# The last two tiles' output product in seven half-size products, and the four narrow tiles' in plain blocks

## The chip, the cores and the metric
The kernel runs on one core of one Trainium2 chip. The metric is the device time of one execution in microseconds (us). Before the change it is 1196.68 us, the median of three runs (1196.1, 1196.68, 1197.64).

## The reference, cut to what matters
```python
# u, v: (8, 3008, 256)   z: (8, 3008, 64)   w_in: (256, 2048)   w_out: (2048, 256)
scores = (1 / 3008) * z @ z.T            # per batch, symmetric
attn = maximum(scores, 0) ** 2
x = u * (attn @ v)                       # 24064 tokens of 256
h = x @ w_in
g = h * cos(h)
out = g @ w_out
```

## The kernel before, in words
The 24064 tokens are cut into 48 tiles, six to a batch, numbered m = 0 to 47. A batch has 3008 = 5 x 512 + 448 tokens, so its sixth tile is short. The 64 tokens left over in an even batch are laid into the last tile of the odd batch after it: tiles 11, 23, 35 and 47 have 512 tokens and tiles 5, 17, 29 and 41 have 384 (`mwidth`, line 393). These four are called narrow here. The inputs of the matmuls are 16-bit floats, the sums 32-bit.

The work goes in slots, s = 3 to 48 (the first three have a form of their own). Slot s has two stages:

- **`phase_a(s)`** (line 305): the scores and the product attn @ v of tile s, as two passes of 47 pairs of matmuls (line 258). The first adds up in the two banks M[0] and M[1] of the accumulator memory, the second in one of the three double banks E[0..2]. ScalarE and VectorE then bring the sums out (`gate_sum`, lines 269 and 270) and VectorE or GpSimd multiplies them by u, which gives x(s) (`gate_mul`, lines 286 and 294). In the last slots no scores are left to do. There is no phase_a(48).
- **`phase_b(s)`** (line 582): eight units of h for tile s-1, with the output product y of tile s-2 between them.

A **unit** of h (`emit_h`, line 396) is four matmuls of 512 columns into the next double bank E, taken in turn (line 403), a sine on ScalarE that gives the cosine c (line 411), and one multiplication h * c on VectorE that writes g and frees the double bank (line 414, here "the g operation"). A unit is two of the 16 blocks of g's depth of 2048. The units go in the order 0, 4, 1, 5, 2, 6, 3, 7, which pairs the upper half of the depth (blocks 0 to 7) with the lower (8 to 15). There are two buffers of g, so g(m) takes the place of g(m-2).

The **output product** has two forms.

- Plain (`emit_y`, line 532; `y_block`, line 522): 16 steps of depth times four blocks of 128 tokens, each one matmul with 256 columns, added up in M[0] and M[1]; `store_y` (line 550) then has ScalarE copy both banks out.
- Mixed (`product`, line 464): the 512 tokens by 2048 of g and the 2048 by 256 of w_out are each cut into 2 x 2 parts, and the result's four quarters are made of seven products of parts or of sums of parts, in place of eight. The sums of w_out's parts are made once (w_mix). Those of g's parts are made per tile: `mix_early` (lines 432 and 433, on GpSimd, one call of two operations for each pair of units) writes s1 and overwrites a quarter of g, and `mix_late` (lines 439 and 441, on VectorE during the next phase_a) writes s2 and s4 in two pieces each. s1, s2 and s4 have one buffer. A product is 16 matmuls of 128 columns (line 482); product n goes to M[0] and M[1] in turn, in the order 5, 1, 6, 7, 2, 3, 4 (`order_y`). Products 5 and 1 are copied out by ScalarE (line 501), each of the others is brought out by one VectorE operation that scales and adds (line 495), and two more sums are made on GpSimd (lines 504 and 507). `store_half` starts the output's DMAs on SyncE's queue: one for a half, or three for the second half of a batch's last tile (lines 542 to 544).

A tile is mixed if 1 <= m < 46. A narrow tile is done with halves of 128 tokens, so its seven products are 8 matmuls each, and its middle 128 tokens go through a plain product of their own (`middle`, line 456, matmuls in line 459). Tiles 0, 46 and 47 are plain. The y of tile 47 is `last_y` (line 561): 64 plain matmuls behind the last unit, two blocks of tokens together and then two one after the other, each with a ScalarE copy (line 571) and a DMA (lines 577 to 580).

Nothing plans the order: the schedule is manual, and each engine runs its instructions as the program emits them. In phase_b a list `after` says behind which unit each product or plain step is emitted. Where y is mixed, a unit's g operation is emitted behind the products that stand with that unit, and so behind their line 495 operations on VectorE; where y is plain, ahead of them. Behind a unit 4 to 7, `mix_early` is emitted.

Of the kernel before, what the change touches and what calls it, by code (L numbers as in the profile page):

```python
# [10 lines left out]
FP32 = mybir.dt.float32  # L11
# [3 lines left out]
def kernel(  # L15
# [9 lines left out]
    nc = tc.nc  # L25
    AF = mybir.ActivationFunctionType
    ALU = mybir.AluOpType

    B, S, D = u.shape
    dqk = z.shape[2]  # L30
    Dff = moe_w_in.shape[1]
    P = 128
    H = P // 2
    CW = 512
# [3 lines left out]
    NFT = Dff // P  # L38
    NSLOT = B * NC
# [4 lines left out]
    inv_s2 = (1.0 / float(S)) * (1.0 / float(S))  # L44
# [16 lines left out]
    opool = pool("o", 2)  # L61
    ypool = pool("ysum", 1)
# [40 lines left out]
    def take_e():  # L103
        i = e_order.pop(0)
        e_order.append(i)
        return i
# [286 lines left out]
    def mwidth(m):  # L393
        return 3 * P if m % (2 * NC) == NC - 1 else CW

    def emit_h(m, i):
        W = mwidth(m)
        x = xs[m]
        e = E[take_e()]
        for f in range(2):  # L400
            ft = 2 * i + f
            for k in range(2):
                nc.tensor.matmul(  # L403
                    e[:, f, 0:W],
                    w_in16[:, k, ft * P:(ft + 1) * P],
                    x[:, k, 0:W],
                    start=(k == 0),
                    stop=(k == 1),
                )
        c = cpool.tile([P, 2, CW], FP16, name="c")  # L410
        nc.scalar.activation(c[:, :, 0:W], e[:, :, 0:W], AF.Sin, bias=half_pi, scale=inv_s2)  # L411
        if m not in gs:
            gs[m] = gpool.tile([P, NFT, CW], FP16, name="g")
        return lambda: nc.vector.scalar_tensor_tensor(  # L414
            gs[m][:, 2 * i:2 * i + 2, 0:W], e[:, :, 0:W], 1.0, c[:, :, 0:W], ALU.mult, ALU.mult
        )

    def mixed(m):
        return 1 <= m < NSLOT - 2

    F = NFT // 2
    T = 2 * P

    def halves_of(m):
        n = T if mwidth(m) == CW else P
        return n, slice(0, n), slice(T, T + n)

    def mix_early(m, j):
        g, f = gs[m], slice(2 * j, 2 * j + 2)
        n, up, low = halves_of(m)  # L430
        lower = slice(F + 2 * j, F + 2 * j + 2)
        nc.gpsimd.tensor_tensor(s1[:, f, 0:n], g[:, f, low], g[:, lower, low], ALU.add)  # L432
        nc.gpsimd.tensor_tensor(g[:, f, low], g[:, f, up], g[:, f, low], ALU.subtract)  # L433

    def mix_late(m, which, c):
        g, f = gs[m], slice(4 * c, 4 * c + 4)
        n, up, low = halves_of(m)
        if which == "s2":
            nc.vector.tensor_tensor(s2[:, f, 0:n], s1[:, f, 0:n], g[:, f, up], ALU.subtract)  # L439
        else:  # L440
            nc.vector.tensor_tensor(  # L441
                s4[:, f, 0:n], g[:, F + 4 * c:F + 4 * c + 4, up], s2[:, f, 0:n], ALU.subtract
            )

    def mix_weights():
# [7 lines left out]

    order_y = (5, 1, 6, 7, 2, 3, 4)

    def middle(m):
        acc = M[0][:, 0:D]
        for ft in range(NFT):
            nc.tensor.matmul(  # L459
                acc, gs[m][:, ft, P:T], w_out16[:, ft, :], start=(ft == 0), stop=(ft == NFT - 1)  # L460
            )
        nc.scalar.activation(y_outs[m][0][:, 1, :], acc, AF.Copy, bias=0.0, scale=inv_s2)

    def product(m, n):
        g = gs[m]
        nk, up, low = halves_of(m)
        nk = nk // P
        t = lambda i: w_mix[:, i, :, :]
        left, right = {
            1: (g[:, 0:F, up], w_out16[:, 0:F, 0:P]),  # L470
            2: (g[:, F:, up], w_out16[:, F:, 0:P]),
            3: (s4, w_out16[:, F:, P:D]),
            4: (g[:, F:, low], t(3)),
            5: (s1, t(0)),
            6: (s2, t(1)),
            7: (g[:, 0:F, low], t(2)),
        }[n]
        at = order_y.index(n) + (nk == 1 and n in order_y[4:])
        acc = M[at % 2][:, 0:nk * P]
        for ft in range(F):  # L480
            for k in range(nk):
                nc.tensor.matmul(  # L482
                    acc[:, k * P:(k + 1) * P],
                    left[:, ft, k * P:(k + 1) * P],
                    right[:, ft, :],
                    start=(ft == 0 and k == 0),
                    stop=(ft == F - 1 and k == nk - 1),
                )
        acc = acc.rearrange("p (k d) -> p k d", d=P)
        if n == 5:  # L490
            y_outs[m] = [opool.tile([P, 2, D], FP32, name="o") for i in range(2)]
            y_parts[m] = {}
        c11, c12, c21, c22 = (y_outs[m][i][:, 0:nk, d * P:(d + 1) * P] for i in range(2) for d in range(2))
        parts = y_parts[m]
        add = lambda dst, other: nc.vector.scalar_tensor_tensor(
            dst, acc, inv_s2, other, ALU.mult, ALU.add
        )
        if n in (1, 5, 6):
            parts[n] = ypool.tile([P, 2, P], FP32, name=f"p{n}")[:, 0:nk, :]
        if n in (1, 5):  # L500
            nc.scalar.activation(parts[n], acc, AF.Copy, bias=0.0, scale=inv_s2)
        elif n == 6:
            add(parts[6], parts[1])
            nc.gpsimd.tensor_tensor(c12, parts[6], parts[5], ALU.add)
        elif n == 7:
            add(c21, parts[6])
            nc.gpsimd.tensor_tensor(c22, c21, parts[5], ALU.add)
        elif n == 2:
            add(c11, parts[1])
        elif n == 3:  # L510
            add(c12, c12)
            store_half(m, 0, y_outs[m][0])
        else:
            add(c21, c21)
            store_half(m, 1, y_outs[m][1])

    def y_bank(m, k):
        if m == NSLOT - 1 and k == 3:
            return E[0][:, 0, 0:D]
        return M[k // 2][:, (k % 2) * D:(k % 2 + 1) * D]  # L520

    def y_block(m, ft, k):
        final = m == NSLOT - 1
        nc.tensor.matmul(  # L524
            y_bank(m, k),
            gs[m][:, ft, k * P:(k + 1) * P],
            w_out16[:, ft, :],
            start=(ft == 0 and (k % 2 == 0 or (final and k == 3))),
            stop=(ft == NFT - 1 and (k % 2 == 1 or k == mwidth(m) // P - 1 or (final and k == 2))),
        )  # L530

    def emit_y(m, i):
# [27 lines left out]

    def last_y(m):
        b, J = m // NC, m % NC
        for ft in range(NFT):
            y_block(m, ft, 0)
            y_block(m, ft, 1)
        for k in range(4):
            if k >= 2:
                for ft in range(NFT):
                    y_block(m, ft, k)
            o = opool.tile([P, 2, D], FP32, name="o")  # L570
            nc.scalar.activation(
                o[:, 0, :], y_bank(m, k),
                AF.Copy, bias=0.0, scale=inv_s2,
            )
            t0 = b * S + J * CW + k * P
            if k < 3:
                nc.sync.dma_start(out[t0:t0 + P, :], o[:, 0, :])
            else:
                nc.sync.dma_start(out[t0:t0 + H, :], o[0:H, 0, :])
                nc.scalar.dma_start(out[b * S - H:b * S, :], o[H:P, 0, :])  # L580

    def phase_b(s):
        y, hs = s - 2, [(s - 1, i) for i in (0, 4, 1, 5, 2, 6, 3, 7)]
        if s == 2:
            hs = [(0, i) for i in range(8)] + hs
        for dh in range(len(late_sums)):
            gate_mul(s, 2 - len(late_sums), late_sums.pop(0), nc.gpsimd)
        if mixed(y):
            ys = [lambda n=n: product(y, n) for n in order_y]
            if mwidth(y) < CW:  # L590
                ys.insert(4, lambda: middle(y))
        else:
            ys = [lambda i=i: emit_y(y, i) for i in range(8)]
            ys[7] = lambda f=ys[7]: (f(), store_y(y))
        n = len(hs)
        if n > 8:
            after = (1, 3, 5, 7, 9, 11, 13, 14)
        elif mixed(y):
            after = (0, 1, 2, 3, 4, 5, 6, 6)
        else:  # L600
            after = (0, 1, 2, 3, 4, 5, 6, 6)
        for i, (m, unit) in enumerate(hs):
            times_c = emit_h(m, unit)
            if not mixed(y):
                times_c()
            for f, place in zip(ys, after):
                if place == i:
                    f()
            if mixed(y):
                times_c()  # L610
            if mixed(m) and unit >= 4:
                mix_early(m, unit - 4)
            if i in (1, 3, 5):
                emit_turns((0, 0), 1)

# [153 lines left out]
```

## Time and profile before

| what | before |
|---|---|
| median of the three runs | 1196.68 us |
| the profiled execution | 1196.1 us |
| its span, first to last instruction | 1194.3 us |
| TensorE matmul busy | 1184.6 us |
| VectorE busy | 1008.6 us |
| ScalarE busy | 795.1 us |
| GpSimd busy | 678.4 us |
| granted TensorE clock | 1.000 |

The span is that of the profiled execution, and 1.8 us lie around it. Busy times of different engines run side by side. PE is TensorE's matmuls, PEld its weight loads, DVE VectorE, ACT ScalarE, POOL GpSimd and SP SyncE, whose queue (SPq) starts most DMAs. In the timelines the columns are start, duration (both us from the span's start), engine, line, operation, output<-inputs with shapes, and a count of instructions merged; the bracket holds the idle time before and what ended it. The stages at the end, from the same execution:

| stage | from to (us) | length |
|---|---|---|
| phase_b(46): h of tile 45, y of 44 | 1133.49 to 1146.76 | 13.27 |
| phase_a(47) | 1146.76 to 1155.76 | 9.00 |
| phase_b(47): h of 46, y of 45 | 1155.76 to 1168.92 | 13.16 |
| phase_b(48): h of 47, y of 46 (plain) | 1168.92 to 1182.98 | 14.06 |
| last_y and the last DMAs | 1182.98 to 1194.30 | 11.32 |

### The profile page before, as it was taken

The numbers are of one execution on the slowest core, as the hardware profiler recorded it, in microseconds if no ns is written. First come the engines' busy times: TensorE is split into PE (matmuls) and PEld (weight loads), VectorE is DVE, ScalarE is ACT, GpSimd is POOL, SyncE is SP. The second block draws the span as 40 slices with busy tenths as digits, with TensorE's granted clock in tenths as the row PEclk, the third lists the DMA queues.
The fourth block names the chain that finished last, engine by engine and source line by source line (L and its number), as shares of the span: only waits on it lengthen the run. The fifth ranks groups of instructions, "written<-read, shape, count | busy, mean of one in ns | idle before, by whom it ended". The sixth has DMA issues, their size and how long they took to land.

```text
span 1194.3 us, 28924 instructions
## 1 busy us (share of the span) xinstructions
PE 1184.6 (99%) x11839; PEld 727.2 (61%) x11839; DVE 1008.6 (84%) x1293; ACT 795.1 (67%) x927; POOL 678.4 (57%) x707
## 2 busy tenths in 40 slices
PE   9899999999999999999999999999999999999998
PEld 4556655665566656566556665666656666665566
DVE  6798988888988898888988889888888888888775
ACT  7866666666766676666766676766766666666454
POOL 3186745557565573665647556476565765545450
PEclk9999999999999999999999999999999999999999
DMA  9999898769995699956999459974798838954301
GB/s 159 172 165 163 121 153 127 118 107 137 139 139 104 114 140 157 128 92 113 150 147 132 91 107 156 169 117 77 121 160 154 122 70 122 183 105 89 65 19 54
DMA packets 479861, 147.98 MB, mean 124 GB/s; under 512 B 404208, under 2 KB 479472, under 8 KB 479728
## 3 DMA queue, kind: packets, MB, share of 16 engines
q1 hardware_dynamic: 380752, 112.93, 54.5%
q0 software_dynamic: 97440, 32.78, 28.1%
q8 instruction: 92, 1.51, 0.5%
q10 hardware_dynamic: 1536, 0.43, 0.2%
q14 instruction: 41, 0.34, 0.1%
HBM read 66.32 MB, written 24.64 MB: 76 GB/s over the span
## 4 chain that ended last, share of the span: by engine, by line
PE 97%; ACT 1%; DVE 1%; issue 1%; ACTq 0%; DVEq 0%
PE E L403 27%; PE M L482 23%; PE M L258 20%; PE E L258 19%; PE E L194 5%; PE M L524 2%; ACT r L204 1%; PE M L459 1%; PE E L654 0%; DVE sm L270 0%; PE E L524 0%; DVE A L209 0%; DVE x L286 0%; DVE g L414 0%; PE M L677 0%
## 5 line engine op out<-in xcount | busy, mean ns | idle before, releaser
L411 ACT ACTIVATE c<-E 128x1024 f16<-128x1024 f32 (+1 forms) x384 | 385.6, 1006 | 218.0 <-PE E L403 214.8
L414 DVE SCALAR_TENSOR_TENSOR g<-E,c 128x1024 f16<-128x1024 f32 (+1 forms) x384 | 458.9, 1197 | 66.7 <-ACT c L411 65.7
L204 ACT ACTIVATE r<-E 128x512 f16<-128x512 f32 (+1 forms) x342 | 327.8, 967 | 114.1 <-PE E L194 108.4
L258 PEld LDWEIGHTS <-v 64*128 64x128 f16 x4512 | 246.8, 94 | 232.4 <-issue 20.6
L403 PE MATMUL E<-x,w_in 128*128 128x512 f16 (+1 forms) x1408 | 353.8, 375 | 0.0
L432 POOL TENSOR_TENSOR s<-g 128x512 f16<-128x512 f16 (+1 forms) x180 | 202.9, 1127 | 185.4 <-DVE g L414 138.9
L258 PE MATMUL M<-A,v 64*128 64x512 f16 (+1 forms) x2256 | 284.9, 372 | 2.1 <-ACT sm L269 1.2
L258 PE MATMUL E<-A,v 64*128 64x512 f16 (+1 forms) x2256 | 279.4, 372 | 0.0
L433 POOL TENSOR_TENSOR g<-g 128x512 f16<-128x512 f16 (+1 forms) x180 | 214.2, 1190 | 14.1
L403 PEld LDWEIGHTS <-w_in 128*128 128x128 f16 x1536 | 133.4, 98 | 108.6 <-issue 19.1
L482 PEld LDWEIGHTS <-g 128*128 128x128 f16 x2752 | 168.6, 98 | 39.8
L209 DVE TENSOR_TENSOR A<-r 128x1024 f16<-128x1024 f16 x240 | 173.3, 734 | 15.1 <-ACT r L204 14.3
L286 POOL TENSOR_TENSOR x<-sm,uT 128x512 f16<-128x512 f32 (+1 forms) x43 | 48.5, 1130 | 214.1 <-DVE sm L270 213.9
L482 PEld LDWEIGHTS <-s 128*128 128x128 f16 x2064 | 126.6, 98 | 30.6
L194 PE MATMUL E<-zT 64*128 64x512 f16 (+4 forms) x684 | 130.0, 356 | 0.5 <-ACT zT L647 0.3
L439 DVE TENSOR_TENSOR s<-s,g 128x1024 f16<-128x1024 f16 (+1 forms) x90 | 98.5, 1094 | 2.1 <-POOL s L432 2.1
L482 PE MATMUL M<-w_out,g 128*128 128x128 f16 x1376 | 91.5, 219 | 0.0
L482 PE MATMUL M<-w_mix,g 128*128 128x128 f16 x1376 | 91.5, 219 | 0.0
L482 PE MATMUL M<-w_mix,s 128*128 128x128 f16 x1376 | 91.5, 219 | 0.0
L212 DVE TENSOR_TENSOR A<-r 128x512 f16<-128x512 f16 (+1 forms) x102 | 80.7, 792 | 10.2 <-ACT r L204 9.4
L194 PEld LDWEIGHTS <-zT 64*128 64x128 f16 x684 | 39.3, 94 | 36.7 <-issue 2.2
L441 DVE TENSOR_TENSOR s<-g,s 128x1024 f16<-128x1024 f16 (+1 forms) x90 | 59.4, 662 | 0.0
(58 smaller groups left out, 657.6 us busy)
## 6 DMA issues: line engine op xcount, KB each, us to landing
out_dram<-o SPq DMA_DIRECT2D x87, 256.0 KB, 2.2
v<-in_v_dram POOLq DMA_DIRECT2D x40, 256.0 KB, 9.2
u<-in_u_dram POOLq DMA_DIRECT2D x40, 256.0 KB, 4.8
A<-A SPq DMA_TRANSPOSE x252, 5.2
z<-in_z_dram POOLq DMA_DIRECT2D x14, 192.0 KB, 10.6
z<-in_z_dram POOLq DMA_DIRECT2D x14, 176.0 KB, 6.3
v<-in_v_dram POOLq DMA_DIRECT2D x8, 192.0 KB, 12.0
u<-in_u_dram POOLq DMA_DIRECT2D x8, 192.0 KB, 4.0
```

The source lines that it names most:

```text
L194: nc.tensor.matmul(e[:, t, 0:Wt], zT[rows, k * P:(k + 1) * P], zT[rows, J * CW:J * CW + Wt], start=True, stop=True,)
L204: nc.scalar.activation(r[:, :, 0:W], e[:, :, 0:W], AF.Relu)
L209: nc.vector.tensor_tensor(a4, r4, r4, ALU.mult)
L212: nc.vector.tensor_tensor(a4, r[:, :, 0:W], r[:, :, 0:W], ALU.mult)
L258: nc.tensor.matmul(bank[:, 0:width(J)], vs[b, k // 4][t * H:(t + 1) * H, k % 4, dh * P:(dh + 1) * P], value_rhs(b, J, k, t), start=start, ...
L403: nc.tensor.matmul(e[:, f, 0:W], w_in16[:, k, ft * P:(ft + 1) * P], x[:, k, 0:W], start=(k == 0), stop=(k == 1),)
L411: nc.scalar.activation(c[:, :, 0:W], e[:, :, 0:W], AF.Sin, bias=half_pi, scale=inv_s2)
L414: return lambda: nc.vector.scalar_tensor_tensor(gs[m][:, 2 * i:2 * i + 2, 0:W], e[:, :, 0:W], 1.0, c[:, :, 0:W], ALU.mult, ALU.mult)
L432: nc.gpsimd.tensor_tensor(s1[:, f, 0:n], g[:, f, low], g[:, lower, low], ALU.add)
L433: nc.gpsimd.tensor_tensor(g[:, f, low], g[:, f, up], g[:, f, low], ALU.subtract)
L439: nc.vector.tensor_tensor(s2[:, f, 0:n], s1[:, f, 0:n], g[:, f, up], ALU.subtract)
L482: nc.tensor.matmul(acc[:, k * P:(k + 1) * P], left[:, ft, k * P:(k + 1) * P], right[:, ft, :], start=(ft == 0 and k == 0), stop=(ft == F - ...
```

## The change
It has four parts.

1. `mixed(m)` now asks for 512 tokens and no longer stops at 46. Tiles 5, 17, 29 and 41 become plain, `halves_of` and `middle` go, and tiles 46 and 47 become mixed.
2. Four of tile 46's units of h (0, 4, 1, 5) move from phase_b(47) to the end of phase_b(46), behind tile 45's eight units and all seven products of tile 44, which read the g buffer that tile 46 takes. phase_b(47) keeps the other four units, with the products of tile 45 two to a unit.
3. The sums of parts of tiles 46 and 47 are emitted by a table `tail`, because there is no later phase_a for them. `mix_early` can run on VectorE. In phase_b(48), product 1 comes ahead of product 5.
4. `last_y` does tile 47 in seven products in the order 1, 2, 4, 5, 7, 6, 3, over six banks of accumulators (M[0], M[1] and two double banks E). Each is brought out by ScalarE or VectorE, with one sum on GpSimd and two on VectorE, and stored in pieces: a quarter behind product 2, the second half (three DMAs on SyncE's queue) behind product 6, and the last quarter in two DMAs, one from SyncE's queue and one from ScalarE's.

```diff
     def mixed(m):
-        return 1 <= m < NSLOT - 2
+        return 1 <= m and mwidth(m) == CW
...
-    def mix_early(m, j):
+    def mix_early(m, j, eng=None):
+        eng = eng or nc.gpsimd
         g, f = gs[m], slice(2 * j, 2 * j + 2)
...
+        eng.tensor_tensor(s1[:, f, :], g[:, f, T:], g[:, lower, T:], ALU.add)
+        eng.tensor_tensor(g[:, f, T:], g[:, f, 0:T], g[:, f, T:], ALU.subtract)
...
+        ea, eb = E[take_e()], E[take_e()]
+        banks = {1: M[1], 2: M[0], 4: ea[:, 0, :], 5: ea[:, 1, :], 7: eb[:, 0, :], 6: eb[:, 1, :], 3: M[1]}
...
+        for n in (1, 2, 4, 5, 7, 6, 3):
+            multiply(m, n, banks[n][:, 0:T])
+            acc = banks[n][:, 0:T].rearrange("p (k d) -> p k d", d=P)
+            if n == 1:
+                copy_to(p[1], acc)
+            elif n == 2:
+                add_to(c11, acc, p[1])
+                nc.sync.dma_start(
+                    out[t0:t0 + T, 0:P].rearrange("(k p) d -> p k d", p=P), c11
+                )
+            elif n == 4:
+                copy_to(c21, acc)
+            elif n == 5:
+                copy_to(p[5], acc)
+                nc.gpsimd.tensor_tensor(c12, p[1], p[5], ALU.add)
+            elif n == 7:
+                add_to(c22, acc, p[1])
+            elif n == 6:
+                add_to(c12, acc, c12)
+                add_to(p[6], acc, c22)
+                nc.vector.tensor_tensor(c22, p[6], p[5], ALU.add)
+                nc.vector.tensor_tensor(c21, p[6], c21, ALU.add)
+                store_half(m, 1, o[1])
             else:
+                for k, eng in enumerate((nc.sync, nc.scalar)):
+                    add_to(c12[:, k, :], acc[:, k, :], c12[:, k, :])
+                    eng.dma_start(out[t0 + k * P:t0 + (k + 1) * P, P:D], c12[:, k, :])
...
+        elif s == NSLOT - 2:
+            hs = hs + [(s, i) for i in (0, 4, 1, 5)]
+        elif s == NSLOT - 1:
+            hs = hs[4:]
...
+        if s == NSLOT - 1:
+            tail = {
+                0: lambda: mix_early(m, 0),
+                1: lambda: mix_early(m, 1),
+                2: lambda: mix_early(m, 2),
+                3: lambda: (mix_early(m, 3, eng=nc.vector), mix_late(m, "s2", 0), mix_late(m, "s2", 1)),
+            }
+        elif s == NSLOT:
+            tail = {
+                1: lambda: (mix_late(y, "s4", 0), mix_late(y, "s4", 1)),
+                3: lambda: (mix_early(m, 0), mix_early(m, 1)),
+                7: lambda: (
+                    mix_early(m, 2, eng=nc.vector), mix_early(m, 3, eng=nc.vector),
+                    mix_late(m, "s2", 0), mix_late(m, "s2", 1),
+                    mix_late(m, "s4", 0), mix_late(m, "s4", 1),
+                ),
+            }
+        if n == 4:
+            after = (0, 0, 1, 1, 2, 2, 3)
+        elif n == 12:
+            after = range(7)
```

More of the change, by code (lines that the diff above doesn't have):

```diff
@@ L418, in mixed @@
     def mixed(m):
-        return 1 <= m < NSLOT - 2
+        return 1 <= m and mwidth(m) == CW
     F = NFT // 2
     T = 2 * P
-    def halves_of(m):
-        n = T if mwidth(m) == CW else P
-        return n, slice(0, n), slice(T, T + n)
-    def mix_early(m, j):
+    def mix_early(m, j, eng=None):
+        eng = eng or nc.gpsimd
         g, f = gs[m], slice(2 * j, 2 * j + 2)
-        n, up, low = halves_of(m)
         lower = slice(F + 2 * j, F + 2 * j + 2)
-        nc.gpsimd.tensor_tensor(s1[:, f, 0:n], g[:, f, low], g[:, lower, low], ALU.add)
-        nc.gpsimd.tensor_tensor(g[:, f, low], g[:, f, up], g[:, f, low], ALU.subtract)
+        eng.tensor_tensor(s1[:, f, :], g[:, f, T:], g[:, lower, T:], ALU.add)
+        eng.tensor_tensor(g[:, f, T:], g[:, f, 0:T], g[:, f, T:], ALU.subtract)
     def mix_late(m, which, c):
         g, f = gs[m], slice(4 * c, 4 * c + 4)
-        n, up, low = halves_of(m)
         if which == "s2":
-            nc.vector.tensor_tensor(s2[:, f, 0:n], s1[:, f, 0:n], g[:, f, up], ALU.subtract)
+            nc.vector.tensor_tensor(s2[:, f, :], s1[:, f, :], g[:, f, 0:T], ALU.subtract)
         else:
             nc.vector.tensor_tensor(
-                s4[:, f, 0:n], g[:, F + 4 * c:F + 4 * c + 4, up], s2[:, f, 0:n], ALU.subtract
+                s4[:, f, :], g[:, F + 4 * c:F + 4 * c + 4, 0:T], s2[:, f, :], ALU.subtract
             )
@@ L454, with multiply @@
     order_y = (5, 1, 6, 7, 2, 3, 4)
[L456 to L464, printed above, removed]
+    def multiply(m, n, acc):
         g = gs[m]
-        nk, up, low = halves_of(m)
-        nk = nk // P
         t = lambda i: w_mix[:, i, :, :]
         left, right = {
-            1: (g[:, 0:F, up], w_out16[:, 0:F, 0:P]),
-            2: (g[:, F:, up], w_out16[:, F:, 0:P]),
+            1: (g[:, 0:F, 0:T], w_out16[:, 0:F, 0:P]),
+            2: (g[:, F:, 0:T], w_out16[:, F:, 0:P]),
             3: (s4, w_out16[:, F:, P:D]),
-            4: (g[:, F:, low], t(3)),
+            4: (g[:, F:, T:], t(3)),
             5: (s1, t(0)),
             6: (s2, t(1)),
-            7: (g[:, 0:F, low], t(2)),
+            7: (g[:, 0:F, T:], t(2)),
         }[n]
-        at = order_y.index(n) + (nk == 1 and n in order_y[4:])
-        acc = M[at % 2][:, 0:nk * P]
         for ft in range(F):
-            for k in range(nk):
+            for k in range(2):
                 nc.tensor.matmul(
@@ L486, in product, with add_to, copy_to @@
                     start=(ft == 0 and k == 0),
-                    stop=(ft == F - 1 and k == nk - 1),
+                    stop=(ft == F - 1 and k == 1),
                 )
+    def add_to(dst, acc, other):
+        nc.vector.scalar_tensor_tensor(dst, acc, inv_s2, other, ALU.mult, ALU.add)
+    def copy_to(dst, acc):
+        nc.scalar.activation(dst, acc, AF.Copy, bias=0.0, scale=inv_s2)
+    def product(m, n, bank):
+        acc = M[bank][:, 0:T]
+        multiply(m, n, acc)
         acc = acc.rearrange("p (k d) -> p k d", d=P)
-        if n == 5:
+        if m not in y_outs:
             y_outs[m] = [opool.tile([P, 2, D], FP32, name="o") for i in range(2)]
             y_parts[m] = {}
-        c11, c12, c21, c22 = (y_outs[m][i][:, 0:nk, d * P:(d + 1) * P] for i in range(2) for d in range(2))
+        c11, c12, c21, c22 = (y_outs[m][i][:, :, d * P:(d + 1) * P] for i in range(2) for d in range(2))
         parts = y_parts[m]
-        add = lambda dst, other: nc.vector.scalar_tensor_tensor(
-            dst, acc, inv_s2, other, ALU.mult, ALU.add
-        )
+        add = lambda dst, other: add_to(dst, acc, other)
         if n in (1, 5, 6):
-            parts[n] = ypool.tile([P, 2, P], FP32, name=f"p{n}")[:, 0:nk, :]
+            parts[n] = ypool.tile([P, 2, P], FP32, name=f"p{n}")
         if n in (1, 5):
-            nc.scalar.activation(parts[n], acc, AF.Copy, bias=0.0, scale=inv_s2)
+            copy_to(parts[n], acc)
         elif n == 6:
@@ L517, in y_bank @@
     def y_bank(m, k):
-        if m == NSLOT - 1 and k == 3:
-            return E[0][:, 0, 0:D]
         return M[k // 2][:, (k % 2) * D:(k % 2 + 1) * D]
     def y_block(m, ft, k):
-        final = m == NSLOT - 1
         nc.tensor.matmul(
@@ L527, in y_block @@
             w_out16[:, ft, :],
-            start=(ft == 0 and (k % 2 == 0 or (final and k == 3))),
-            stop=(ft == NFT - 1 and (k % 2 == 1 or k == mwidth(m) // P - 1 or (final and k == 2))),
+            start=(ft == 0 and k % 2 == 0),
+            stop=(ft == NFT - 1 and (k % 2 == 1 or k == mwidth(m) // P - 1)),
         )
@@ L562, in last_y @@
         b, J = m // NC, m % NC
[L563 to L577, printed above, removed]
-            else:
-                nc.sync.dma_start(out[t0:t0 + H, :], o[0:H, 0, :])
-                nc.scalar.dma_start(out[b * S - H:b * S, :], o[H:P, 0, :])
+        t0 = b * S + J * CW
+        ea, eb = E[take_e()], E[take_e()]
+        banks = {1: M[1], 2: M[0], 4: ea[:, 0, :], 5: ea[:, 1, :], 7: eb[:, 0, :], 6: eb[:, 1, :], 3: M[1]}
+        o = [opool.tile([P, 2, D], FP32, name="o") for i in range(2)]
+        c11, c12, c21, c22 = (o[i][:, :, d * P:(d + 1) * P] for i in range(2) for d in range(2))
+        p = {n: ypool.tile([P, 2, P], FP32, name=f"p{n}") for n in (1, 5, 6)}
+        for n in (1, 2, 4, 5, 7, 6, 3):
[21 more added lines that the diff above has]
+                store_half(m, 1, o[1])
+            else:
+                for k, eng in enumerate((nc.sync, nc.scalar)):
+                    add_to(c12[:, k, :], acc[:, k, :], c12[:, k, :])
+                    eng.dma_start(out[t0 + k * P:t0 + (k + 1) * P, P:D], c12[:, k, :])
     def phase_b(s):
@@ L588, in phase_b @@
         if mixed(y):
-            ys = [lambda n=n: product(y, n) for n in order_y]
-            if mwidth(y) < CW:
-                ys.insert(4, lambda: middle(y))
+            ys = [
+                lambda n=n, i=i: product(y, n, i % 2)
+                for i, n in enumerate(order_y if s < NSLOT else (1, 5) + order_y[2:])
+            ]
         else:
@@ L595, in phase_b @@
         n = len(hs)
-        if n > 8:
+        m = s - 1
+        tail = {}
+        if s == NSLOT - 1:
[19 more added lines that the diff above has]
+            after = range(7)
+        elif n > 8:
             after = (1, 3, 5, 7, 9, 11, 13, 14)
         elif mixed(y):
-            after = (0, 1, 2, 3, 4, 5, 6, 6)
+            after = range(7)
         else:
             after = (0, 1, 2, 3, 4, 5, 6, 6)
-        for i, (m, unit) in enumerate(hs):
-            times_c = emit_h(m, unit)
+        for i, (mh, unit) in enumerate(hs):
+            times_c = emit_h(mh, unit)
             if not mixed(y):
@@ L610, in phase_b @@
                 times_c()
-            if mixed(m) and unit >= 4:
-                mix_early(m, unit - 4)
+            if mixed(mh) and unit >= 4 and mh < NSLOT - 2:
+                mix_early(mh, unit - 4)
+            if i in tail:
+                tail[i]()
             if i in (1, 3, 5):
```

## The prediction
> **What bounds the kernel now.** I read the page's busy line and its chain first, then timelines: the ordinary phase_b, a narrow tile's, and the end.
>
> ```profile
> PE 1184.6 (99%) x11839; PEld 727.2 (61%) x11839; DVE 1008.6 (84%) x1293; ACT 795.1 (67%) x927; POOL 678.4 (57%) x707
> ...
> PE 97%; ACT 1%; DVE 1%; issue 1%; ACTq 0%; DVEq 0%
> ```
>
> TensorE is busy for 1184.6 of 1194.3 us and carries 97% of the chain, so a matmul more or less counts in full, and any wait that TensorE does not have yet is a loss. The 9.7 us that it idles lie at the start, before it has data, and behind its last matmul (4.3 us, below). An ordinary unit with its product, in the timeline of phase_b(47):
>
> ```profile
> 1161.04 1.03 PE L403 MATMUL E<-x,w_in 128*128 128x512 f16 x4
> 1161.31 0.42 DVE L495 SCALAR_TENSOR_TENSOR p<-M,p 128x256 f32<-128x256 f32 x1
> 1161.65 1.21 DVE L414 SCALAR_TENSOR_TENSOR g<-E,c 128x1024 f16<-128x1024 f32 x1
> ...
> 1161.90 1.06 PE L482 MATMUL M<-w_mix,g 128*128 128x128 f16 x16
> 1162.10 1.02 ACT L411 ACTIVATE c<-E 128x1024 f16<-128x1024 f32 x1 [0.73 <-PE E L403]
> ...
> 1162.79 1.03 PE L403 MATMUL E<-x,w_in 128*128 128x512 f16 x4
> ```
>
> Take starts, not durations, since matmuls overlap: a unit costs TensorE 0.87 (1161.04 to 1161.90), a product 0.89 (1161.90 to 1162.79), or 55.5 ns for each of 16 matmuls. The cosine starts 1.06 behind its unit and takes 1.02. On VectorE the next operation starts 0.34 behind a line 495 one (1161.31 to 1161.65) and about 1.18 behind a g operation (elsewhere two in a row take 2.36). Per unit VectorE then needs 1.5 of 1.75: it keeps up, with little room.
>
> **Part 1, the narrow tiles.** The same phase for tile 41:
>
> ```profile
> 1068.33 1.91 PE L459 MATMUL M<-w_out,g 128*128 128x256 f16 x16
> ...
> 1070.07 1.03 PE L403 MATMUL E<-x,w_in 128*128 128x512 f16 x4
> ...
> 1072.69 0.61 PE L482 MATMUL M<-w_mix,g 128*128 128x128 f16 x8
> ...
> 1073.14 1.03 PE L403 MATMUL E<-x,w_in 128*128 128x512 f16 x4
> ...
> 1074.10 1.47 PE L258 MATMUL M<-A,v 64*128 64x512 f16 x12
> ```
>
> A half product of 8 matmuls takes 0.445 (1072.69 to 1073.14), the middle's 16 take 1.74 (1068.33 to 1070.07), 108.5 ns each. Now: 7 x 0.445 + 1.74 = 4.85. Plain: 48 matmuls x 108.5 ns = 5.21. Each narrow tile costs 0.36 more. VectorE and GpSimd lose the sums of these tiles, which saves nothing: TensorE is busy for all of the 11.89 us of this phase. A wait is added. A plain y ends with two ScalarE copies of M[0] and M[1], behind the cosine of the seventh unit, and the next phase_a writes both banks one unit (0.87) later. The one place where the trace shows this order, tile 0 ahead of phase_a(3), has the copies end at 75.07 while TensorE was there at 74.70, about 0.4 lost. Here the second copy is half as wide and the y matmuls ahead end later, so I take 0.15, with ends 0 and 0.4. Four tiles: 4 x (0.36 + 0.15) = **+2.0** (1.45 to 3.1).
>
> A rule speaks against products of 128 columns altogether. The Trainium skill (TensorE: Matmul & The Clock Gate, section Back-to-back issue gap) gives about 81 ns per matmul for a sustained stream of weight loads and matmuls at 128 columns, and 109 ns for 256 by its formula. By it a wide tile would take 9.1 mixed and 7.0 plain, and a narrow one 6.3 and 5.2: the two wide tiles would lose 4.2 and the four narrow ones gain 4.2. The rows above show 55.5 ns, and the sum goes by them.
>
> **Part 2, five units in a row.** At the end of phase_b(46) unit 7 of tile 45 and four units of tile 46 stand without a product between. TensorE needs 0.87 for each, VectorE 1.18, and there are three double banks, so a unit waits for the g operation three units before. Count from the start of unit 3 of tile 45, whose g operation ends about 3.6 later, as for the same unit of tile 46 in the trace (1166.31, g at 1168.67 for 1.22). The five units would start at 1.75, 2.62, 3.49, 4.36 and 5.23. The third waits until 3.6. The fourth needs the first's g operation, which starts with its cosine's end at 1.75 + 1.06 + 1.02 = 3.83 and ends at 5.05. The fifth needs the second's, 1.18 later. It starts at 6.25, **+1.0** (0.3 to 1.5). phase_a(47) then doesn't wait: its second pass takes the double bank of the fifth unit, but only 4.4 later. The same four units go from phase_b(47), for nothing else.
>
> **Part 3, y of tile 46.** Mixed, 7 x 0.89 = 6.21, in place of plain, 64 x 108.5 ns = 6.94: **-0.73**. VectorE's work grows, though. From the last g operation of tile 46 to that of tile 47 it has 9 g operations (10.4), 5 of line 495 (1.7), one `mix_early` (two of 512, about 0.34 each by the row above for the same time per element) and four pieces of s2 and s4 (two in a row take 1.28, so 0.64 each, 2.5): 15.3. TensorE takes 15.0 over the same units and products. So VectorE is the full engine here, some tenths of it come back through the double banks and M: **+0.15** (0 to 0.6).
>
> **Part 4, the end.**
>
> ```profile
> 1181.95 1.03 PE L403 MATMUL E<-xodd,w_in 128*128 128x512 f16 x4
> ...
> 1182.82 5.40 PE L524 MATMUL M<-w_out,g 128*128 128x256 f16 x48
> ...
> 1188.06 1.91 PE L524 MATMUL E<-w_out,g 128*128 128x256 f16 x16
> 1190.05 0.39 ACT L571 ACTIVATE o<-E 128x256 f32<-128x256 f32 x1 [0.87 <-PE E L524]
> 1190.46 0.51 SPq L579 DMA_DIRECT2D out_dram<-o  x1
> ```
>
> Now last_y runs without a gap from the last unit's end (1182.98, the start of the 48 in the chain of waits) to 1189.98, one copy follows, and the last DMA is issued at 1190.46: 7.5 behind the last unit. The g operation of that unit ends 2.4 behind it, hidden under the first 24 matmuls.
>
> After: that g operation still ends 2.4 to 2.6 behind the unit, and only then can VectorE make the sums of units 2, 6, 3 and 7 and s2 and s4, all in its own queue: 4 x 0.34 + 4 x 0.64 = 3.9, to 6.5. Meanwhile TensorE waits twice, for the g operation of unit 3 (about 0.9 in product 1) and of unit 7 (0.3 in product 2), and ends at 6.2 + 1.2 = 7.4. VectorE's queue holds product 2's sum behind the sums of g. So six operations remain from 6.5 on, two for products 2 and 7, two for product 6, and two sums, 0.34 each: 8.6. Then the second half's three DMAs go to SyncE's queue, ahead of one of the last two:
>
> ```profile
> 343.09 0.34 SPq L542 DMA_DIRECT2D out_dram<-o  x1
> 343.49 0.54 SPq L543 DMA_DIRECT2D out_dram<-o  x1
> 344.08 0.58 SPq L544 DMA_DIRECT2D out_dram<-o  x1
> ```
>
> They hold the queue for 1.57, so the last one is issued at 10.2, **+2.7** against 7.5, the matmuls saved included. Ends: 1.3, if the three don't hold the last DMA and its own sum is what it waits for, and 3.6, if each of the six operations waits for the one before (0.15 each). What follows the last issue (3.84 to the span's end) is taken as the same. One more price: two operations that read on-chip memory on both VectorE and GpSimd delay each other.
>
> ```profile
> 102.06 1.26 POOL L432 TENSOR_TENSOR s<-g 128x512 f16<-128x512 f16 x1 [0.55 <-DVE g L414]
> 102.23 1.64 DVE L439 TENSOR_TENSOR s<-s,g 128x1024 f16<-128x1024 f16 x1
> ...
> 103.41 1.49 POOL L433 TENSOR_TENSOR g<-g 128x512 f16<-128x512 f16 x1
> ```
>
> VectorE's operation took 1.64, not 0.64 to 0.69, since GpSimd had begun. At the end GpSimd's one sum of products 1 and 5 (0.73, line 504's row) falls beside the last pieces of s2 and s4. It costs 0 or 0.73: **+0.4**.
>
> **The sum.** 2.0 + 1.0 - 0.73 + 0.15 + 2.7 + 0.4 = +5.5 on the profiled execution's 1196.1 (span 1194.3 and 1.8 around it): **1201.6**. That execution is the fastest of three, 0.6 below their median, so a median could be 0.6 higher. With all low ends 1198.4, with all high ends 1204.8.
>
> **Rivals.**
>
> - *A wash (not slower).* Only matmuls count: 4 x 0.36 lost, 2 x 0.73 won, sum 0, **1196.1**. It needs VectorE not to matter at the end. For it: GpSimd and ScalarE are idle there, and TensorE has seven products of cover. Against: the sums of g's last units depend on the last unit, and VectorE makes them alone. It decides if the chain behind the last unit is under 8.2.
> - *Slower still, VectorE bound from phase_b(47) on.* GpSimd's `mix_early` for tile 46 runs beside VectorE's sums there, and every late g operation holds a double bank. If each of the six VectorE sums of 0.64 or more ran at 1.64, some 6 more minus what is counted: **1205 to 1207**. Against it: by my count GpSimd is done there when VectorE begins.
> - *Faster.* The relief of VectorE and GpSimd in the four narrow tiles would free TensorE. All idle time but the end's is 9.7 - 4.3 = 5.4, so at most 1196.1 - 5.4 = **1190.7**; but the narrow phase shows TensorE without a gap.
> - That the change does nothing isn't open: the matmul counts differ.
>
> **How the numbers follow.** My forecast 0.74, the wash 0.13, slower still 0.10, faster 0.03. The forecast's own range is 1198.4 to 1204.8. I take in a little of the neighbours, 1197.6 to 1205.0, which leaves out about 0.18. About 0.2% (2.4 us) is what a measurement of this kernel can tell from no change. From the cases: faster 0.03; same 0.15, the wash and the lowest edge of the forecast; slower 0.82.
>
> **What would show it.** Narrow phases: 48 plain matmuls, 12.2 to 12.5 long, not 11.89. phase_b(46): the last units of h 1.2 apart, not 0.87. The end: TensorE's last matmul about 7.4 behind the last unit, and 2 to 3 us between it and SyncE's last DMA, with VectorE busy in between. I am wrong if VectorE is idle behind the last unit's g operation, or if that last DMA is issued within 9 us of the last unit.

## The result, and the profile after

The changed kernel takes 1202.1 us, the median of four runs (1201.34 to 1202.91), against 1196.62 for the kernel before, four runs. The ratio is 1.0045, with a 95% interval of 1.0027 to 1.0062: slower by some 5.5 us. The forecast was 1201.6.

The profiled execution after took 1202.7, with a span of 1200.9, 6.6 more than before. Not all of that is the change: executions of one kernel fall into two groups, 1.2 to 1.5 apart (within each group the two kernels differ by 4.9 and 5.2), and the two profiles lie in different ones. What differs is TensorE's granted clock for a few us early on. The windows answer (busy time of PE, PEld, DVE, ACT and POOL, each with its number of instructions, then the granted clock, the DMA share and GB/s) shows the stretch from 40 to 45 us before, and then after:

```profile
40.00:45.00 5.00, 5.00 (x49) 2.97 (x47) 3.34 (x5) 5.00 (x6) 0.47 (x1) 1.00 1.08 154
```
```profile
40.00:45.00 5.00, 5.00 (x35) 2.29 (x32) 2.24 (x4) 3.79 (x5) 0.26 (x1) 0.69 1.07 151
```

With a mean clock of 0.69 (0.50 in the two us from 40 to 42 alone) 35 matmul records fit where 49 stood, and the first narrow phase, at 183.44 before, starts at 184.77, ahead of anything that the change touches: 1.33 later. So I read the rest by stages, which this doesn't disturb. The page after:

```profile
PE 1187.2 (99%) x11839; PEld 735.6 (61%) x11839; DVE 1007.0 (84%) x1284; ACT 795.0 (66%) x922; POOL 666.0 (55%) x680
...
PE 96%; DVE 2%; ACT 1%; issue 1%; DVEq 0%; ACTq 0%
```

TensorE still carries the chain, but VectorE's share went from 1% to 2%. Where, the timelines tell. First the narrow tile 41's phase, its start before:

```profile
1062.21 1.04 PE L403 MATMUL E<-x,w_in 128*128 128x512 f16 x4
```

and its start and end after:

```profile
1064.75 1.04 PE L403 MATMUL E<-x,w_in 128*128 128x512 f16 x4
...
1074.73 1.47 PE L512 MATMUL M<-w_out,g 128*128 128x256 f16 x12
1076.04 1.03 PE L403 MATMUL E<-x,w_in 128*128 128x512 f16 x4
1077.00 1.51 PE L258 MATMUL M<-A,v 64*128 64x512 f16 x12
```

The next phase_a starts at 1077.00 (before, at 1074.10), so this phase is 12.25 long and not 11.89: the 48 plain matmuls. The phase_a behind it takes 11.42 (11.38 before), so the wait for the copies of M is 0.04. In all, phase_b(44) starts 2.94 later than before; without the 1.33 that is 1.61, or 0.40 for each narrow tile. Then the units in a row of phase_b(46):

```profile
1148.74 2.90 PE L403 MATMUL E<-x,w_in 128*128 128x512 f16 x12
...
1152.14 2.15 PE L403 MATMUL E<-x,w_in 128*128 128x512 f16 x8 [0.50 <-DVE g L414]
...
1154.22 4.71 PE L258 MATMUL M<-A,v 64*128 64x448 f16 x47
```

Three units fit the double banks. The last two wait for VectorE's g operations, named in the bracket. From the first of the five units to phase_a(47) it takes 5.48 and not 4.43 (four units of 0.87 and the 0.96 that the last unit before a phase_a takes), and the phase takes 17.79: 13.27 as before, 3.47 for four units, 1.05 of waiting. Then phase_b(48), whose first unit starts before at

```profile
1168.92 1.03 PE L403 MATMUL E<-xodd,w_in 128*128 128x512 f16 x4
```

and whose first and last units start after at

```profile
1172.94 1.03 PE L403 MATMUL E<-xodd,w_in 128*128 128x512 f16 x4
...
1185.38 1.03 PE L403 MATMUL E<-xodd,w_in 128*128 128x512 f16 x4
```

Last, the end after (some of its PE, DVE, POOL and SPq lines; lines 465, 474 and 477 of the kernel after are the matmuls of a product, VectorE's scale-and-add and ScalarE's copy):

```profile
1187.73 1.53 PE L465 MATMUL M<-w_out,g 128*128 128x128 f16 x20 [0.65 <-DVE g L414]
...
1190.62 1.05 PE L465 MATMUL E<-w_mix,s 128*128 128x128 f16 x16 [0.47 <-ACT o L477]
1191.51 1.29 DVE L436 TENSOR_TENSOR s<-g,s 128x1024 f16<-128x1024 f16 x2
...
1192.17 1.21 POOL L571 TENSOR_TENSOR o<-p,p 128x256 f32<-128x256 f32 x1 [4.53 <-ACT p L477]
...
1193.52 1.05 PE L465 MATMUL E<-w_mix,s 128*128 128x128 f16 x16 [0.95 <-DVE o L474]
1194.41 1.06 PE L465 MATMUL M<-w_out,s 128*128 128x128 f16 x16
1194.68 0.42 DVE L474 SCALAR_TENSOR_TENSOR o<-E,o 128x256 f32<-128x256 f32 x1 [1.21 <-PE E L465]
...
1195.88 0.42 DVE L578 TENSOR_TENSOR o<-p,o 128x256 f32<-128x256 f32 x1
...
1197.29 0.59 SPq L532 DMA_DIRECT2D out_dram<-o  x1
1198.00 0.51 SPq L583 DMA_DIRECT2D out_dram<-o  x1
```

The brackets on PE lines are TensorE's waits. The first is the one for g of unit 3. The second and third stand in front of products 5 and 6, and name the operations that bring out products 4 and 7, which share a double bank with them. VectorE makes the last pieces of s4 until 1192.80, then brings out products 2 and 7, waits 1.21 for product 6 (its bracket), makes that product's sums until 1196.30, and only then do the second half's three DMAs and the last DMA go out.

By stages, counting a unit of h from the start of its first matmul to 0.87 behind the start of its four (which puts the last unit's end before at 1182.82):

| step | before | after | difference |
|---|---|---|---|
| span's start to the first narrow phase (lower clock) | 183.44 | 184.77 | +1.33 |
| four narrow tiles | | | +1.61 |
| phase_b(46) and (47) together | 26.43 | 27.51 | +1.08 |
| phase_b(48), to the last unit's end | 13.90 | 13.31 | -0.59 |
| last unit's end to the span's end | 11.48 | 14.65 | +3.17 |
| span | 1194.3 | 1200.9 | +6.6 |

Without the first row the change's own part is 5.3.

### The profile page after: what moved, and what is told of

It reads as the page before. It is cut to its first block, busy times and chain, and to the rows that moved or that the text cites. A ratio compares the mean times of both kernels' runs of the same rounds, so it can differ in the third digit from the quotient of the medians.

```text
span 1200.9 us, 28851 instructions
## 1 busy us (share of the span) xinstructions
PE 1187.2 (99%) x11839; PEld 735.6 (61%) x11839; DVE 1007.0 (84%) x1284; ACT 795.0 (66%) x922; POOL 666.0 (55%) x680
## 4 chain that ended last, share of the span: by engine, by line
PE 96%; DVE 2%; ACT 1%; issue 1%; DVEq 0%; ACTq 0%
PE E L403 27%; PE M L465 22%; PE M L258 20%; PE E L258 19%; PE E L194 5%; PE M L512 2%; ACT r L204 1%; DVE g L414 1%; PE E L687 0%; DVE sm L270 0%; DVE o L474 0%; DVE A L209 0%; DVE x L286 0%; DVE s L434 0%; DVE A L212 0%
## 5 line engine op out<-in xcount | busy, mean ns | idle before, releaser
L258 PEld LDWEIGHTS <-v 64*128 64x128 f16 x4512 | 254.2, 94 | 227.0 <-issue 23.4
L428 POOL TENSOR_TENSOR s<-g 128x512 f16<-128x512 f16 x169 | 197.2, 1167 | 172.7 <-DVE g L414 129.8
L429 POOL TENSOR_TENSOR g<-g 128x512 f16<-128x512 f16 x169 | 208.1, 1231 | 13.3
L434 DVE TENSOR_TENSOR s<-s,g 128x1024 f16<-128x1024 f16 x86 | 95.7, 1116 | 1.0 <-POOL s L428 1.0
L465 PE MATMUL M<-w_mix,g 128*128 128x128 f16 x1344 | 88.7, 219 | 0.0
L465 PE MATMUL M<-w_mix,s 128*128 128x128 f16 x1344 | 88.7, 219 | 0.0
L436 DVE TENSOR_TENSOR s<-g,s 128x1024 f16<-128x1024 f16 x86 | 58.6, 685 | 0.0
```

The source lines that it names most:

```text
L258: nc.tensor.matmul(bank[:, 0:width(J)], vs[b, k // 4][t * H:(t + 1) * H, k % 4, dh * P:(dh + 1) * P], value_rhs(b, J, k, t), start=start, ...
L428: eng.tensor_tensor(s1[:, f, :], g[:, f, T:], g[:, lower, T:], ALU.add)
L429: eng.tensor_tensor(g[:, f, T:], g[:, f, 0:T], g[:, f, T:], ALU.subtract)
L434: nc.vector.tensor_tensor(s2[:, f, :], s1[:, f, :], g[:, f, 0:T], ALU.subtract)
L465: nc.tensor.matmul(acc[:, k * P:(k + 1) * P], left[:, ft, k * P:(k + 1) * P], right[:, ft, :], start=(ft == 0 and k == 0), stop=(ft == F - ...
```

## The experiments

All are told by the same stages; the times are medians beside runs of the kernel before on the same chip.

**Part 1 alone.** The kernel before with

```diff
-        return 1 <= m < NSLOT - 2
+        return 1 <= m < NSLOT - 2 and mwidth(m) == CW
```

> The kernel before with part 1 alone: tiles 5, 17, 29 and 41 plain, tiles 46 and 47 plain as before. Theory (each narrow tile costs 0.36 of matmuls and up to 0.15 of a wait): 1.4 to 2.0 us slower than before, each narrow phase_b about 12.25 long instead of 11.89 and the next phase_a up to 0.05 longer. Rival (the sums that VectorE and GpSimd lose give time back to TensorE): at most 0.5 slower.

1199.05 against 1196.65, ratio 1.0015 (1.0006 to 1.0024). The narrow phase is 12.25 long, the end as before (11.5 from the last unit). Its profile has the early stretch of low clock too (the first narrow phase starts at 184.76), and phase_b(43), phase_b(44) and phase_b(46) start within 0.01 of where they start after: the 1.6 is shown, and the rest of the 2.4 between the medians goes with that clock. The sums that VectorE and GpSimd are spared give nothing back.

**Parts 2 to 4 alone.** The kernel after with `mixed` for every m >= 1, and `halves_of` and `middle` kept, so that narrow tiles are mixed as before.

> Parts 2 to 4 alone: tiles 46 and 47 mixed with the moved units and the new last_y, narrow tiles mixed as before. Theory (the loss is mostly at the end): 3.0 to 4.0 us slower than before; with the part-1 kernel's loss it sums to the whole change. Rival (the whole change's loss is in the narrow tiles, or in the lower clock early in the profiled execution after): within 1 of before.

1201.73, ratio 1.0035 (1.0022 to 1.0048). phase_b(46) 17.79, phase_b(48) 13.31, 14.67 from the last unit to the end: the three terms of after, 3.7 in sum. The rival falls. The medians lie 5.1 apart and not 3.7, mostly because four of its five executions have a mean clock of 0.997 or 0.998.

**Products of tile 47 dealt out otherwise over the double banks.**

```diff
-        banks = {1: M[1], 2: M[0], 4: ea[:, 0, :], 5: ea[:, 1, :], 7: eb[:, 0, :], 6: eb[:, 1, :], 3: M[1]}
+        banks = {1: M[1], 2: M[0], 4: ea[:, 0, :], 5: eb[:, 0, :], 7: ea[:, 1, :], 6: eb[:, 1, :], 3: M[1]}
```

> The kernel after, with the four products of tile 47 that lie in double banks dealt out as 4 and 7 in one and 5 and 6 in the other, in place of 4 and 5, 7 and 6. Theory (product 5 waits for the copy of 4, and product 6 for VectorE's sum of 7, only because they share a double bank): 1.0 to 1.3 us less than after, product 6 starts on the heels of 7. Rival (product 6 waits for its operand s2, or VectorE's chain is full anyway): within 0.3 of after, and the wait stays, put down to s2.

1201.98, ratio 1.0041 (1.0027 to 1.0055); all five executions have a mean clock of 0.997, so the median doesn't show the gain. From the last unit to the end it takes 13.8, not 14.65: 0.85 less, a little under the theory's 1.0. Both waits are gone, products 5, 7 and 6 follow each other:

```profile
1191.56 1.82 DVE L436 TENSOR_TENSOR s<-g,s 128x1024 f16<-128x1024 f16 x2
1191.59 1.24 POOL L571 TENSOR_TENSOR o<-p,p 128x256 f32<-128x256 f32 x1 [3.91 <-ACT p L477]
1191.82 1.06 PE L465 MATMUL E<-w_mix,s 128*128 128x128 f16 x16
1192.71 1.34 PE L465 MATMUL M<-w_out,s 128*128 128x128 f16 x16
```

So the two products waited for nothing but the other half of their double bank; whether the chip or only the program's own bookkeeping asks for that wait, the runs don't show. What they show next is the second line: GpSimd's sum now starts 0.03 behind the first piece of s4 and takes 1.24, not 0.73, and the second piece takes 1.22, not 0.69, so that the two take 1.82 and not 1.29. That is the price of 0.53 that the prediction had put at 0.4; it was not paid in the kernel after, where GpSimd's sum came beside the second piece and only waited itself (1.21).

**The last quarter's two DMAs on one queue.**

```diff
-                for k, eng in enumerate((nc.sync, nc.scalar)):
+                for k, eng in enumerate((nc.scalar, nc.scalar)):
```

> The kernel after, with both DMAs of the last quarter on ScalarE's queue, none of them behind the second half's three DMAs on SyncE's. Theory (the three hold the last one back): SyncE's last DMA is the third of the half, at about 11.0 behind the last unit instead of 11.75, and the end is 0.5 to 0.9 earlier than after. Rival (the drain behind the last issue is what counts, the order of issue doesn't): within 0.2 of after.

1201.59, ratio 1.0041 (1.0028 to 1.0053). The rival holds: SyncE's last DMA goes out 0.72 earlier, as expected, and the end comes 14.60 behind the last unit, 0.05 less than after. But what the rival calls the drain is no fixed time either: the span ends 3.6 behind the last issue here and 2.9 after. In the six kernels with the new `last_y` it ends 4.51 to 4.62 behind VectorE's last sum for the second half, whichever DMA is issued last. What sets these 4.6 is not shown.

**Part 2 alone.** The kernel before with the two new branches for `hs` (four units moved) and the new `after` lists, tiles 46 and 47 plain.

> The kernel before with part 2 alone: units 0, 4, 1 and 5 of tile 46 at the end of phase_b(46), the other four in phase_b(47) with tile 45's products two to a unit; tiles 46 and 47 stay plain. Theory (five units in a row run at VectorE's pace): phase_b(46) takes 3.5 for the units and 1.0 to 1.1 of waiting, nothing comes back in phase_b(47), 1.0 to 1.1 slower than before. Rival (the double banks' backlog is made good later, or two products to a unit lose time): under 0.4, or over 1.6, slower.

1197.54 against 1196.79, ratio 1.0008 (1.0000 to 1.0017). phase_b(46) 17.79, phase_b(47) 9.71, the rest as before: 1.05 lost, as the theory has it. (The medians are 0.75 apart.) With products two to a unit phase_b(47) loses nothing.

**Parts 3 and 4 without the move.** The two branches for `hs` go, `mix_early` of tile 46 runs on GpSimd as for other tiles, and s2 and s4 of tile 46 are made behind units 0 and 4 of tile 47.

> Tiles 46 and 47 mixed with the new last_y, narrow tiles mixed as before, but no unit moved: mix_early of tile 46 runs on GpSimd behind its units as for other tiles, s2 and s4 are made on VectorE behind the first two units of tile 47. Theory: what the kernel with parts 2 to 4 loses, less the 1.1 of the moved units: about 2.3 to 2.8 slower than before, with the last unit 0.5 to 0.75 earlier than before and 14.6 from its end to the span's end. Rival (the move was needed: s2 comes late and products 5 and 6 of tile 46 wait): phase_b(48) 14.0 or longer, no better than with the move.

1200.4, ratio 1.0031 (1.0019 to 1.0042). Here the rival was right: phase_b(48) is 14.24 long instead of 13.31, with waits in front of products 5 and 6 that the next kernel shows. The move costs 1.05 and buys 0.93, so it is nearly even. From the last unit to the end, 14.59.

**Tile 46 mixed alone.** The same schedule with the `last_y` of before for tile 47.

> The kernel before with tile 46 mixed and nothing moved; tile 47 plain with the last_y of before. Theory: it has the 0.73 of tile 46 and none of the losses: phase_b(48) 13.2 to 13.6 long instead of 14.06, 11.3 from the last unit's end to the span's end as before, in all 0.4 to 0.7 faster than before, too little for the timed runs to show. Rival (VectorE is the full engine in phase_b(48)): no gain, phase_b(48) 13.9 or longer.

1196.99, ratio 1.0004 (0.9995 to 1.0013). Again my theory fell: phase_b(48) takes 14.24 and the rest to the end 11.70, 0.56 slower than before by the stages. Two lines of its timeline say why (line 481 holds a product's matmuls):

```profile
1174.14 0.40 PE L481 MATMUL M<-w_mix,s 128*128 128x128 f16 x4 [0.32 <-POOL s L433]
...
1176.25 0.62 PE L481 MATMUL M<-w_mix,s 128*128 128x128 f16 x8 [0.40 <-DVE s L440]
```

Products 5 and 6 wait in the middle for the last pieces of s1 and s2. The rival had the number but not the cause; that called for the last two kernels.

**All mended that had shown itself.** No move, the double banks dealt out as above, and the second half's DMAs from ScalarE's, SyncE's and ScalarE's queue.

> The kernel without a moved unit, with tile 47's products dealt out over the double banks as 4 and 7, 5 and 6, and the second half's three DMAs shared by ScalarE's and SyncE's queues. Theory (the double banks cost 0.85, the queue some 0.5): 1.3 less than the kernel without a moved unit, 12.9 to 13.5 from the last unit's end to the span's end, still 1.0 to 1.5 slower than before, because VectorE's chain behind the last unit stays. Rival (the queue is not in the chain): 13.8, as with the banks alone.

1200.09, ratio 1.0025 (1.0016 to 1.0034): 13.64 from the last unit to the end, 0.95 less than without the mends and 2.2 more than before. By the kernel with the double banks alone they are 0.85 of the 0.95 and the queues 0.1, so it lies nearer the rival's 13.8. VectorE's sums behind the last unit stay; with the `last_y` of before in their place (the kernel with tile 46 mixed alone) the same stretch took 11.70.

**Tile 46 with its raw products first.** The products that need no sum of parts of g (1, 2, 4) come first, then 5, 7, 6, 3; s2 and s4 are made behind units 1 and 5 of tile 47, which come third and fourth.

```diff
...
+                ys = [
+                    lambda n=n, i=i: product_raw(y, n, (i + 1) % 2)
+                    for i, n in enumerate((1, 2, 4, 5, 7, 6, 3))
+                ]
...
```

> Tile 46 mixed and nothing moved, as in the kernel with tile 46 alone, but its products in the order 1, 2, 4, 5, 7, 6, 3: the three that read g as it is come first, and s1, s2 and s4 are needed two to four units later. Tile 47 plain with the last_y of before. Theory (phase_b(48) lost the 0.7 of tile 46 only because products 5 and 6 stood there before their sums were made): phase_b(48) 13.2 to 13.4 long, no wait for s1 or s2, 0.6 to 0.8 faster than before among executions with the same early clock. Rival (VectorE is full in phase_b(48) with or without waits for sums): 13.9 or longer, or the time comes back as a wait at the start of last_y.

1196.45 against 1197.54, ratio 0.9994 (0.9985 to 1.0004). Theory and rival are half right each. phase_b(48) is 13.16 long, the bare matmuls, so waiting for sums was the cause. But the time comes back at once, as 12.22 from the last unit to the end in place of 11.48 (line 564 is the plain matmul of `y_block`):

```profile
1182.38 1.47 PE L564 MATMUL M<-w_out,g 128*128 128x256 f16 x12
...
1184.39 4.11 PE L564 MATMUL M<-w_out,g 128*128 128x256 f16 x36 [0.54 <-DVE g L414]
```

`last_y` goes through the depth from block 0 on, and unit 3, the last but one to be made, holds blocks 6 and 7. VectorE is a unit late by then.

**The same, with `last_y` in the order of the units.**

```diff
-        for ft in range(NFT):
-            y_block(m, ft, 0)
-            y_block(m, ft, 1)
+        for i in (0, 4, 1, 5, 2, 6, 3, 7):
+            for ft in (2 * i, 2 * i + 1):
+                y_block(m, ft, 0)
+                y_block(m, ft, 1)
```

> The kernel with tile 46's raw products first, and last_y's first two blocks over the depth in the order in which the units of tile 47 are done (0, 4, 1, 5, 2, 6, 3, 7) in place of 0 to 7. Theory (the wait of 0.7 for unit 3's g at the start of last_y was what took back tile 46's 0.7): no wait there, TensorE's last matmul 20.3 to 20.4 behind the start of phase_b(48) instead of 21.06 before, 0.6 to 0.8 faster than before among executions with the same early clock. Rival (the last unit's g operation is late as well): a wait of 0.3 or more stays in front of unit 7, under 0.4 faster.

```profile
1171.15 1.03 PE L403 MATMUL E<-xodd,w_in 128*128 128x512 f16 x4
...
1184.31 5.50 PE L564 MATMUL M<-w_out,g 128*128 128x256 f16 x48
```

The 48 matmuls run without the wait; they begin 13.16 behind the start of phase_b(48), and 11.59 later the span ends. That is 24.75 against 25.38 before: 0.63 faster. The median is 1196.77 against 1197.63, ratio 0.9993 (0.9984 to 1.0002), so the medians alone don't settle it. The stages do, and the executions agree with them: the five of the lower group take 1195.19 to 1195.60, the six of the kernel before 1196.01 to 1196.28 (in the upper groups it is 1196.77 to 1197.12 against 1197.58 to 1197.87, with two executions of the new kernel outside, at 1197.70 and 1198.75). It is the one kernel here that is faster than the one before by its stages, and it takes from the change only the mixed tile 46.

## Why the prediction was right, point by point

- **Narrow tiles, +2.0.** Measured 1.61. The matmuls were right (0.36 each). The wait for the copies of M, put at 0.15, is 0.04. The place it was taken from, tile 0, had two full copies; here the second is half as wide. The about 81 ns that the Trainium skill (TensorE: Matmul & The Clock Gate, section Back-to-back issue gap) gives for a matmul of 128 columns do not hold for this stream: phase_b(48) with seven mixed products and nothing to wait for takes 13.16, which is 8 x 0.87 and 7 x 0.89, or 55.5 ns a matmul.
- **Five units in a row, +1.0.** Measured 1.05, after and alone.
- **Tile 46, -0.73 + 0.15.** Measured -0.59. What I didn't see is that with products 5 and 1 first this gain hangs on the move: without it the sums are late and the gain is gone.
- **The end, +2.7 and +0.4.** Measured +3.17 against 3.1, but that they agree so well is luck: terms were off and hid each other. To the last DMA's issue it is 11.75 - 7.64 = 4.1, not 2.7. The six VectorE operations counted there started as forecast, 6.46 behind the last unit (forecast 6.5), but ran to 10.05, not 8.6. The wait in between was not in the prediction: product 6 waited for VectorE to bring out product 7 from the same double bank, and VectorE then stood idle for 1.21 until product 6 was there. Counted by starts, TensorE lost 2.8 in four waits, not 1.2 in two, and its last matmul ends some 9.1 behind the last unit, not 7.4. Idle time of VectorE behind the last g operation was a sign I had named for being wrong, and here I was. Against that, what follows the last issue is 2.9 and not the 3.84 that I took as the same, and the delay of VectorE by GpSimd was nil, not 0.4. I had made the queue of three DMAs part of the path, with 1.57; putting the last DMA elsewhere moved the end by 0.05. The step that held is the one that decides: VectorE's sums of the last units can't start before the last g operation.
- **The rivals.** The wash would have needed the chain behind the last unit to end within 8.2; VectorE's last sum ends at 10.05, and the stretch is 3.2 longer than before. VectorE is full in phase_b(48) (13.04 of 13.31 busy), but GpSimd's `mix_early` didn't slow its sums of tile 46, as I had counted: both pairs of pieces of s2 and s4 take 1.29. The relief of VectorE and GpSimd in narrow phases frees nothing (part 1 alone).

The sum of the stages is 5.3, and 5.5 was forecast: the parts held, but inside the end the waits and the sizes did not.

## What to carry to other kernels

A form of a product that saves multiplications but needs sums of its operand is paid for where nothing follows: at the last tile 0.73 of matmuls were saved, and VectorE's sums (4.1, from 1188.70 to 1192.80) and late additions (3.6, to 1196.30, with 1.21 of waiting among them) came to stand in the open. One tile earlier the same form gave 0.6 of its 0.73, once the products that need no sum came first. With VectorE near full there, the wait that was removed came back at the next place that read its newest result, until the order of reading followed the order of making.

## What the runs showed of the hardware

- In some executions of a kernel TensorE's granted clock falls to half for some us. Of the twelve profiles here, six show it at 38 to 44 us and one at 56 to 62, all with 0.50 in the lowest window of 2 us; in them the first narrow phase starts at 184.76 to 185.66, in the other five at 183.44 to 183.78. Of 15 executions of the kernel before, beside the last experiment, 6 had a mean clock of 1.000 and took 1196.01 to 1196.28, and 9 had 0.998 or 0.999 and took 1197.58 to 1197.87. Elsewhere the mean tells them apart less well: beside the first experiments, three with 0.999 took 1195.78 to 1196.15. TensorE is busy for 0.78 us of the 2 us from 36 to 38 in the profile before and for 0.63 in the one after, and only in the latter does the fall follow; what decides is not shown.
- VectorE and GpSimd operations that both read two operands from on-chip memory take turns: a GpSimd sum that came beside the last of two pieces of s4 took 1.21, not 0.73, and the two pieces 1.29; one that came beside the first piece took 1.24, and the two pieces 1.82. The Trainium skill (SBUF — State Buffer, section SBUF: two separate sides) says that the two share a port pair, that whichever operation starts first holds it for the whole instruction, and that the other blocks. Both rows agree with that: in both GpSimd waits some 0.5 for the piece that has begun, and in the second the next piece waits 0.53 for GpSimd.
